# DMA transposes for the q and k of the last four groups, and a different pairing of score blocks from pair 12, in an attention-then-MLP kernel

## The chip, the core and the metric

One core of one Trainium2 chip runs the whole program. The metric is the device time of one execution in microseconds; less is better. TensorE (PE in the profile) does the matrix products, VectorE (DVE), ScalarE (ACT) and GpSimd (POOL) do the elementwise work, and all DMAs are issued by SyncE (SP), whose queue is worked off in order. Each engine runs its own instructions strictly in the order in which they were written; semaphores join the engines.

## What is computed

Attention of two kinds, added, for 8 batches of 8 heads with 576 tokens and head size 64; then an MLP whose activation is h - tanh(h), over 4608 tokens.

```
q_d, k_d, v_d = mean over 4 neighbouring tokens of q, k, v      # 144 coarse tokens
out_d   = softmax(scale * q_d k_d^T) v_d ;  out_up = repeat(out_d, 4)
mask    = |i - j| < 4
out_loc = softmax(where(mask, scale * q k^T, -1e9)) v
x = (out_up + out_loc) as [4608, 512]
h = x @ w_in          # 512 -> 2048
out = (h - tanh(h)) @ w_out    # 2048 -> 512
```

## The kernel before

**Units of work.** Two heads make a pair (p = 0 to 31), two pairs a group (n = 0 to 15), four pairs a batch. The MLP runs over blocks of 512 tokens (kb = 0 to 8) and can begin on a block when the four pairs of its batch or batches have been written into `xT`.

**A group's q and k.** `load_qk` brings them token-major into `qkn` (L345). `reorder` casts them to bf16 into `qr` (L441, q on DVE and k on POOL from group 2 on). `turn(n, i)` (i = 0 for q, 1 for k) then needs the head dimension on the partitions: nine 128x128 transposes on PE (L457) into the PSUM bank pair `ts`, and one ACT copy (L463) from there into `qk`. Two POOL additions (L473, L478) make the coarse version `qkd`. `qr`, `qk` and `qkd` have two buffers each, by n % 2.

**A pair's attention** (`attention(p)`, a generator whose three segments are emitted at different places). `s1` is eight score products of the fine attention in `ts`; `s2` is the two remaining fine ones and four coarse ones. Up to pair 13 they are two PE operations, both in `ts`; from `MERGE` = 14 on one PE operation does `s1` and `s2` of the same pair, `s1` in `ts` and `s2` in the other bank pair `ox`. ACT takes the exponentials (L547 for `s1`, L562 and L565 for `s2`), DVE multiplies by the mask (L551, L569), PE forms the outputs in `ox` (L580, L586), DVE normalises into `ln` (L595, L597). Up to pair 11 PE turns `ln` back (L631 to L635). From `XOUT` = 12 on SP issues a DMA transpose of `ln` into `lnT` (L605; 128 x 896 bf16, seven blocks of 128x128), and DVE adds from there into `xT` (L616).

**The MLP.** `mm1` (L663) and `mm2` (L691) work in four PSUM banks `ps_hy`; ACT's tanh (L672) and DVE's subtraction (L675) lie between them. ACT copies the results (L702) into three buffers `y`, and SP stores them (L705).

**What sets the order.** Nothing is scheduled by hand. `Program` collects the operations with the keys that they read and write, a cost in ns and a priority (lower goes first: attention has 10 or 20 times its number, the MLP's products have 5000). `order()` then plays the program through once with those costs. The latency `LAT` of the producing engine, plus what `spare` adds for late priorities, separates a result from its reader on another engine. The instructions are emitted in the order of these planned starts. So the costs are no work on the chip; they decide the order in which each engine's queue is written, and for a `choice` the engine as well. Where PE is planned to be idle before the first MLP block, a `filler` issues dummy products (L869).

**Loads.** `load_next` runs after each odd pair. A load waits for its buffer and for the key `fl` of pair 2n - `AHEAD`, which the transposes of L605 write, so only loads from about group 9 on wait for it. `vst` has `NVST` = 6 buffers for v, taken by p % 6.

Of the kernel before, what the change touches and what calls it, by code (L numbers as in the profile page):

```python
# [9 lines left out]
BF16 = mybir.dt.bfloat16  # L10
# [5 lines left out]
class Program:  # L16
# [10 lines left out]
    def __init__(self):  # L27
        self.ops = []
        self.alternatives = {}
        self.touch = []  # L30
        self.fresh = set()
        self.spare = (5000, {})
        self.last_write = {}
        self.readers = {}

# [26 lines left out]
    def order(self):  # L62
        n = len(self.ops)
        users = [[] for _ in range(n)]
        left = [0] * n
        for i, (_, _, _, deps, _) in enumerate(self.ops):
            left[i] = len(deps)
            for d in deps:
                users[d].append(i)
        at = [0.0] * n  # L70
        free, ready, start = {}, {}, [None] * n

        def make_ready(i):
            for eng in self.alternatives.get(i, (self.ops[i][0],)):
                ready.setdefault(eng, []).append(i)
        for i in range(n):
            if left[i] == 0:
                make_ready(i)
        for _ in range(n):
            best = None  # L80
            for eng, cand in ready.items():
                if not cand:
                    continue
                now = max(free.get(eng, 0.0), min(at[i] for i in cand))
                if eng == "DMA":
                    pick = min((at[i], i) for i in cand)[1]
                else:
                    pick = min((self.ops[i][4], i) for i in cand if at[i] <= now)[1]
                if best is None or now < best[0]:
                    best = (now, eng, pick)  # L90
            now, eng, i = best
            if i in self.alternatives:
                for other in self.alternatives[i]:
                    ready[other].remove(i)
                self.ops[i] = self.alternatives[i][eng] + self.ops[i][3:]
            else:
                ready[eng].remove(i)
            start[i] = now
            end = now + self.ops[i][1]
            free[eng] = end  # L100
            for u in users[i]:
                same = self.ops[u][0] == eng and eng != "DMA"
                lag = self.LAT[eng]
                if self.spare[0] <= self.ops[u][4] < 5000:
                    lag += self.spare[1].get(eng, 0)
                at[u] = max(at[u], end if same else end + lag)
                left[u] -= 1
                if left[u] == 0:
                    make_ready(u)
        self.start, self.free = start, free  # L110
        return sorted(range(n), key=lambda i: (start[i], i))
# [43 lines left out]
def kernel(  # L155
# [9 lines left out]
    nc = tc.nc  # L165
# [3 lines left out]
    NP = H // 2  # L169
# [4 lines left out]
    A6 = 9  # L174
# [65 lines left out]
        ps_hy.extend(fixed("ps_hy", [128, 512], FP32, 4, pool=pool))  # L240

    P = Program()
    P.spare = (140, {"DMA": 2500, "POOL": 1000})
    op = P.op
    V, A, T, GP = nc.vector, nc.scalar, nc.tensor, nc.gpsimd

# [48 lines left out]
    def load(ns, fn, keys, cost, pri, after=()):  # L295
        op("SP", ns, fn, reads=after, writes=list(keys) + ["queue", ("q", keys[0])],
           pri=pri)
        op("DMA", cost, None, reads=[("q", keys[0])], writes=keys, pri=pri)

    def slot_qk(n):  # L300
        return n % 2 if n >= GV else n % NQKN

    def load_v4(n):

        b, h0 = n // 2, 4 * (n % 2)
        base = v[b, h0]
        for i, (g0, m) in enumerate(((0, 128), (128, 16))):
            rows = bass.AP(tensor=base.tensor, offset=base.offset + 4 * D * g0,
                           ap=[[4 * D, m], [S * D, 4], [1, 4 * D]])
            to = v4[128 - m:128, i]  # L310
            load(650, lambda to=to, rows=rows: nc.sync.dma_start(out=to, in_=rows),
                 [("qkn", 2, i, y) for y in range(2)], (1100, 350)[i], -30,
                 [("fl", 2 * n - AHEAD)])

    def sum_v(n):
# [16 lines left out]
    def load_qk(n):  # L332

        b, h0, s = n // 2, 4 * (n % 2), slot_qk(n)
        for i, src in enumerate((q, k)):
            for y in range(2):
                base = src[b, h0 + 2 * y]
                rows = bass.AP(tensor=base.tensor, offset=base.offset,
                               ap=[[A6 * D, G6], [S * D, 2], [1, A6 * D]])
                t = qkn[s][:, i]  # L340
                to = bass.AP(tensor=t.tensor, offset=t.offset + y * t.ap[0][0],
                             ap=[[2 * t.ap[0][0], G6], t.ap[1], t.ap[2]])

                def issue(to=to, rows=rows):
                    nc.sync.dma_start(out=to, in_=rows)  # L345
                load(650, issue, [("qkn", s, i, y)], T_QK, -30,
                     [("fl", 2 * n - AHEAD)])

    def load_v(p):

        b, j, s = p // NP, p % NP, p % NVST
        t = vst[s]
        for i in range(2):
            h = 2 * j + i
# [22 lines left out]
    def load_w(src, dst, name, f, stage, keys):  # L377

        def issue():
# [4 lines left out]
            else:  # L384
# [4 lines left out]
                else:  # L389
                    nc.sync.dma_start(  # L390
                        out=stage.rearrange("p (c f) -> p c f", c=4),
                        in_=rows[:, 4 * f:4 * f + 4, :])
        load(600, issue, keys, T_W, -30)
        for c in range(4):
            part = stage[c] if isinstance(stage, list) else stage[:, 512 * c:512 * c + 512]
            to = dst[:, c, 512 * f:512 * f + 512] if src is moe_w_in else dst[:, 4 * f + c, :]
# [3 lines left out]


    def prep_v(p):
        s, w, jj = p % NVST, (p // 2) % NVW, p % 2
        P.choice([(eng, ns, lambda fn=fn: fn(  # L404
            out=vw[w][:, 2 * jj:2 * jj + 2, :, 0:64], in_=vst[s]))
                  for eng, ns, fn in CAST_V[p >= NEARLY]],
                 reads=[("vst", s, 0), ("vst", s, 1)],
                 writes=[("vw", w, jj)], pri=10 * p - 12)

    def pool_v(hb):  # L410
# [6 lines left out]
        def mm():  # L417
# [5 lines left out]
        P.fresh.add(len(P.ops))  # L423
        op("PE", 750, mm, reads=[("vw", w, 0), ("vw", w, 1), "pick"],
           writes=[key], pri=pri)
        op("ACT", 300, lambda: A.copy(
            out=vd[w][:, :, :, 0:64],
            in_=pv.rearrange("p w (h d) -> p w h d", d=D)),
           reads=[key], writes=[("vd", w)], pri=pri)
# [16 lines left out]
    def turn(n, i):  # L446
# [4 lines left out]
            ps, ts = po, ox  # L451
        pri, cold = 20 * n, (1.5 if n < 1 else 1.0)
        b16 = ps.rearrange("p n c -> p (n c)").bitcast(BF16)[:, 0:A6 * 128]

        def tr():
            for a in range(A6):
                T.transpose(b16[:, 128 * a:128 * a + 128], qr[s][:, i, a, :], ident)  # L457
        P.fresh.add(len(P.ops))
        op("PE", 480 * cold, tr, reads=[("qr", s, i), "ident"], writes=ts, pri=pri)
        o = qk[s][:, :, KOFF * i:KOFF * i + 576]  # L460

        def copy(fn):
# [13 lines left out]
        def add2(eng):  # L476
            with nc.allow_low_precision("pooled q and k"):
# [3 lines left out]
                 reads=[("qk", s, i)], writes=["half"], pri=pri)  # L481
        P.choice([(name, n2, lambda eng=eng: add2(eng)) for name, _, n2, eng in adders],
                 reads=["half"], writes=[("qkd", s, i)], pri=pri)

    def attention(p):
        b, j, hb, s, jj = p // NP, p % NP, p // 2, p % 2, p % 2
# [41 lines left out]
                             pT[rows, 0, y, :], start=True, stop=True)  # L528
        qks = [("qk", sq, i) for i in range(2)]
        pad = ["bias", "ident"] if first else []  # L530
        yield
        P.fresh.add(len(P.ops))
        if first:
            op("PE", 480, lambda: off(0, 480, 0), reads=pad, writes=ts, pri=pri)
        qkds = [("qkd", sq, i) for i in range(2)]
        if p >= MERGE:
            def both():
                s1()
                s2()
            op("PE", 800, both, reads=qks + qkds, writes=ts + ox, pri=pri)  # L540
        else:
            op("PE", 420 * cold, s1, reads=qks, writes=ts, pri=pri)
        se = p if p < NP else s
        e1 = E[se][:, 0:960].rearrange("p (h c) -> p h c", h=2)
# [3 lines left out]
            out=e1, in_=ps[:, :, 0:480], func=AF.Exp, scale=SCALE),  # L548
           reads=ts, writes=[("E", se, 0)], pri=pri)
        if not first:  # L550
            op("DVE", 700, lambda: V.tensor_tensor(  # L551
                out=e1, in0=e1,
                in1=mask[:, 0:480].unsqueeze(1).to_broadcast([128, 2, 480]),
                op=ALU.mult), reads=["mask"], writes=[("E", se, 0)], pri=pri)
# [1 line left out]
        P.fresh.add(len(P.ops))  # L556
        if first:
            op("PE", 100, lambda: off(480, 96, 0), reads=pad, writes=ts, pri=pri)
        if p < MERGE:
            op("PE", 380 * cold, s2, reads=qks + qkds, writes=ts, pri=pri)  # L560
        sb = ox if p >= MERGE else ts
        op("ACT", 335, lambda: A.activation(  # L562
            out=e2v, in_=pb[:, :, 0:96], func=AF.Exp, scale=SCALE),
# [2 lines left out]
            out=e3, in_=pb[:, :, 96:384], func=AF.Exp, scale=SCALE / 16.0),  # L566
           reads=sb, writes=[("E", se, 2)], pri=pri)
        if not first:
            op("DVE", 220, lambda: V.tensor_tensor(  # L569
                out=e2v, in0=e2v,  # L570
                in1=mask[:, 480:576].unsqueeze(1).to_broadcast([128, 2, 96]),
                op=ALU.mult), reads=["mask"], writes=[("E", se, 1)], pri=pri)
# [109 lines left out]
    def mm2(kb, i):  # L682
# [16 lines left out]
        if part == 3:  # L699
# [5 lines left out]
            op("SP", 600, lambda: nc.sync.dma_start(  # L705
                out=out[r0:r0 + 128, :], in_=y[ys]),
               reads=[("y", ys)], writes=[("yq", ys)], pri=-1)
            op("DMA", 1000, None, reads=[("yq", ys), ("y", ys)], pri=-1)

    def dense(kb):  # L710

# [12 lines left out]
        for i in range(16):  # L724
            if kb < NBLK:
# [2 lines left out]


    M2_FIRST = 16  # L730
    XOUT, T_OUT, AHEAD = 12, 2000, 5
    MERGE, GV = 14, 7
    XADD = [("DVE", (800, 350), V)]
    ORDER, W_FIRST = "g0123", "0123g"
    INNER, OUTER = {4: [0], 5: [1]}, {3: [0, 1], 7: [0, 1]}
    T_QK, T_V, T_W, W_PRI, NEARLY = 760, 800, 2750, 33, NP
    CAST = [("POOL", 700, GP.tensor_copy), ("ACT", 520, A.copy)]
    CAST_V = [[("POOL", 720, GP.tensor_copy), ("ACT", 640, A.copy)],
              [("POOL", 790, GP.tensor_copy)]]
    any3 = [("DVE", 860, V.tensor_copy), ("ACT", 950, A.copy),  # L740
            ("POOL", 1350, GP.tensor_copy)]
    REORDER = [[any3, any3], [any3[0:1], any3[2:3]]]
    TURN = [[("ACT", 1125, A.copy), ("DVE", 1250, V.tensor_copy)],
            [("ACT", 1125, A.copy)]]
    ADDERS = [[("DVE", 750, 440, V), ("POOL", 1190, 750, GP)],
              [("POOL", 1190, 880, GP)]]

    op("DVE", 180, lambda: V.memset(warm, 0.0), writes=["warm"], pri=-999)
# [87 lines left out]
    for p in range(NPAIR):  # L836
# [4 lines left out]
            prep_v(p + 2)  # L841
        if p >= 2:
            next(work[p])
        inner = INNER.get(p, [p % 2] if p >= 2 * NP else [])
        outer = OUTER.get(p, [])
        for i in inner if n + 1 < NGRP else []:
            reorder(n + 1, i)
            turn(n + 1, i)
        next(work[p], None)
        for i in outer:  # L850
            reorder(n + 1, i)
            turn(n + 1, i)
        if p % 2 == 1:
            load_next()
        if p % NP == NP - 1:
# [45 lines left out]
```

## Time and profile before

| what | value |
|---|---|
| median of 6 runs | 345.37 us (344.33 to 346.21) |
| the profiled execution | 344.93 us, span 343.2 us |
| mean granted PE clock in it | 0.984 |
| PE busy | 323.0 us, 94% |
| DVE, ACT, POOL busy | 214.2, 204.6, 152.5 us |
| DMA queue of the loads and stores | 60.1% of the 16 engines' span |
| L663 and L691, both MLP products | 144.2 and 142.0 us busy |
| L457, the transposes of q and k | 252 recorded into `ts`, 19.1 us busy; 36 into `ox`, 3.6 us |

Busy time of a group is the time covered by its instructions from start to end, so groups that overlap are counted in both. PE's instructions are pipelined: the next starts before the one before has ended, and the mean length of an instruction is more than the time it takes from PE. What an instruction takes from PE is read from the distance between starts.

### The profile page before, as it was taken

To read this page: it belongs to the slowest core of one execution; us is meant where nothing else is said; L and a number is where in the kernel's file an instruction comes from. 1 tells how busy PE (TensorE), PEld (TensorE's weight loads), DVE (VectorE), ACT (ScalarE), POOL (GpSimd) and SP (SyncE) were. 2 spreads that over 40 slices of the span, in tenths; PEclk is the share of its full clock that TensorE was granted. 3 is DMA by queue.
4 is the path that set the end of the run, shared out by engine and by line. 5 is a ranking of instruction groups with operands and counts; after the bars stand their busy time and mean duration, and the time that the engine had idled before them with its cause. 6 is when DMAs were issued, how large, how long until landed. Compare 5 with 4: busy or idle time off the path is not lost.

```text
span 343.2 us, 6786 instructions
## 1 busy us (share of the span) xinstructions
PE 323.0 (94%) x2570; PEld 168.6 (49%) x2616; DVE 214.2 (62%) x360; ACT 204.6 (60%) x342; POOL 152.5 (44%) x179
## 2 busy tenths in 40 slices
PE   5977998988999999999999999999999999999995
PEld 1563554554555554555455555454544444444442
DVE  4774765549987678678787568776676453344300
ACT  2685986568868665766666656665765244344411
POOL 8445847595795065839393739493300000000000
PEclk9698999999999999999999999999999999999999
DMA  6999999999902496879878868862222200100021
GB/s 221 269 389 290 273 348 286 270 292 275 265 4 58 127 274 186 215 191 208 226 175 215 185 185 215 227 171 59 59 57 60 57 31 32 61 31 32 31 85 67
DMA packets 84749, 57.51 MB, mean 168 GB/s; under 512 B 62638, under 2 KB 67822, under 8 KB 84718
## 3 DMA queue, kind: packets, MB, share of 16 engines
q1 hardware_dynamic: 84718, 57.09, 60.1%
q8 instruction: 20, 0.33, 0.4%
q14 instruction: 11, 0.09, 0.1%
HBM read 43.05 MB, written 9.44 MB: 153 GB/s over the span
## 4 chain that ended last, share of the span: by engine, by line
PE 80%; DMA 7%; DVE 3%; ACT 3%; SPq 3%; issue 2%; POOL 1%; POOLq 0%; DVEq 0%; ACTq 0%
PE ps_hy L663 34%; PE ps_hy L691 32%; PE ps_ts L457 3%; DMA qkn<-in_q_dram 3%; DMA qkn<-in_k_dram 3%; PE ps_ts L508 3%; PE ps_ox L580 3%; PE ps_ox L586 2%; SPq L345 1%; DMA vst<-in_v_dram 1%; SPq L369 1%; ACT E L547 1%; DVE ln L597 1%; DVE xT L640 1%; PE ps_ox L419 1%
## 5 line engine op out<-in xcount | busy, mean ns | idle before, releaser
L663 PE MATMUL ps_hy<-xT,w_in_sb 128*128 128x512 bf16 x555 | 144.2, 382 | 4.6 <-DVE xT L640 2.7
L691 PE MATMUL ps_hy<-w_out_sb,gT 128*128 128x512 bf16 x552 | 142.0, 379 | 2.4 <-issue 1.1
L675 DVE TENSOR_TENSOR gT<-ps_hy,uy 128x512 bf16<-128x512 f32 x144 | 95.7, 685 | 57.5 <-ACT uy L672 56.7
L672 ACT ACTIVATE uy<-ps_hy 128x512 f32<-128x512 f32 x144 | 83.6, 600 | 78.6 <-PE ps_hy L663 76.6
L663 PEld LDWEIGHTS <-w_in_sb 128*128 128x128 bf16 x576 | 53.7, 98 | 62.7 <-issue 5.9
L691 PEld LDWEIGHTS <-gT 128*128 128x128 bf16 x576 | 53.4, 98 | 60.5 <-issue 1.4
L473 POOL TENSOR_TENSOR half<-qk 128x576 f32<-128x576 bf16 x29 | 34.6, 1195 | 56.8 <-ACT qk L463 55.7
L463 ACT COPY qk<-ps_ts 128x1152 bf16<-128x1152 bf16 x28 | 31.5, 1126 | 14.8 <-PE ps_ts L457 12.6
L702 ACT COPY uy<-ps_hy 128x512 f32<-128x512 f32 x36 | 21.2, 588 | 22.5 <-PE ps_hy L691 20.7
L597 DVE TENSOR_TENSOR ln<-ps_ox,r 128x896 bf16<-128x896 f32 x30 | 32.7, 1089 | 0.9
L547 ACT ACTIVATE E<-ps_ts 128x960 bf16<-128x960 f32 x30 | 29.2, 973 | 6.8 <-PE ps_ts L508 6.7
L404 POOL CAST vw<-vst 128x640 bf16<-128x640 f32 x31 | 24.6, 805 | 10.6 <-DMA vst<-in_v_dram 3.8
L551 DVE TENSOR_TENSOR E<-E,mask 128x960 bf16<-128x960 bf16 x28 | 21.9, 780 | 11.7 <-ACT E L547 11.4
L457 PEld LDWEIGHTS <-qr 128*128 128x128 bf16 x288 | 19.5, 102 | 12.3 <-DVE qr L441 5.5
L322 POOL TENSOR_TENSOR qkn<-qkn 128x512 f32<-128x512 f32 (+1 forms) x18 | 23.9, 1327 | 3.0 <-DMA qkn<-in_v_dram 1.6
L441 DVE CAST qr<-qkn 128x1152 bf16<-128x1152 f32 x18 | 14.2, 790 | 14.7 <-DMA qkn<-in_q_dram 12.2
L478 POOL TENSOR_TENSOR qkd<-half 128x288 bf16<-128x288 f32 x30 | 21.6, 721 | 2.3 <-DVE half L473 1.3
L457 PE MATMUL ps_ts<-ident,qr 128*128 128x128 bf16 x252 | 19.1, 222 | 3.0 <-POOL vd L765 1.5
L441 POOL CAST qr<-qkn 128x1152 bf16<-128x1152 f32 x14 | 17.0, 1218 | 10.3 <-DMA qkn<-in_k_dram 9.8
L616 DVE TENSOR_TENSOR xT<-lnT 128x480 bf16<-128x480 bf16 (+1 forms) x40 | 21.3, 545 | 0.0
L580 PE MATMUL ps_ox<-vw,E 128*128 128x65 bf16 x300 | 18.3, 194 | 1.5 <-DVE E L569 1.5
L595 DVE RECIPROCAL r<-ps_ox 128x14 f32<-128x14 f32 x30 | 7.3, 243 | 19.6 <-PE ps_ox L586 17.7
(86 smaller groups left out, 253.2 us busy)
## 6 DMA issues: line engine op xcount, KB each, us to landing
vst<-in_v_dram SPq DMA_DIRECT2D x62, 160.0 KB, 5.3
qkn<-in_q_dram SPq DMA_DIRECT2D x32, 288.0 KB, 3.4
qkn<-in_k_dram SPq DMA_DIRECT2D x32, 288.0 KB, 5.0
out_dram<-uy SPq DMA_DIRECT2D x36, 256.0 KB, 2.1
qkn<-in_v_dram SPq DMA_DIRECT2D x9, 512.0 KB, 5.0
gT<-in_moe_w_in_dram SPq DMA_DIRECT2D x4, 1024.0 KB, 9.8
xT<-in_moe_w_out_dram SPq DMA_DIRECT2D x8, 256.0 KB, 5.2
gT<-in_moe_w_out_dram SPq DMA_DIRECT2D x2, 1024.0 KB, 10.1
```

The costliest lines, as they stand in the source:

```text
L404: P.choice([(eng, ns, lambda fn=fn: fn(out=vw[w][:, 2 * jj:2 * jj + 2, :, 0:64], in_=vst[s])) for eng, ns, fn in CAST_V[p >= NEARLY]], rea ...
L441: P.choice([(eng, ns, lambda fn=fn: fn(out=dst, in_=srt)) for eng, ns, fn in REORDER[n >= 2][i]], reads=[("qkn", sn, i, x) for x in range(2)],
L457: T.transpose(b16[:, 128 * a:128 * a + 128], qr[s][:, i, a, :], ident)
L463: fn(out=o.rearrange("p y (g a) -> p y g a", a=A6), in_=b16.rearrange("p (a g y) -> p y g a", a=A6, y=2))
L473: eng.tensor_tensor(out=half, in0=four[:, :, :, 0:2], in1=four[:, :, :, 2:4], op=ALU.add)
L547: op("ACT", 980, lambda: A.activation(out=e1, in_=ps[:, :, 0:480], func=AF.Exp, scale=SCALE), reads=ts, writes=[("E", se, 0)], pri=pri)
L580: T.matmul(po[:, hh, 65 * t:65 * t + 65], E[se][:, c:c + 128], vw[w][:, 2 * jj + hh, t, :], start=True, stop=True)
L597: op("DVE", 1090, lambda: V.tensor_tensor(out=ln[sl].rearrange("p n (h d) -> p h n d", d=D), in0=blocks[:, :, :, 0:64], in1=r[s].unsqueeze ...
L663: T.matmul(ps_hy[slot], w_in_sb[:, dc, fc * 128:(fc + 1) * 128], xT[dc][:, kb * 512:kb * 512 + 512], start=(dc == 0), stop=(dc == N_DC - 1))
L672: op("ACT", 490, lambda: A.activation(out=u[us], in_=ps_hy[slot], func=AF.Tanh), reads=[("hy", slot)], writes=[("u", us)], pri=-1)
L675: op("DVE", 620, lambda: V.tensor_tensor(out=gT[g][:, fc, :], in0=ps_hy[slot], in1=u[us], op=ALU.subtract), reads=[("hy", slot), ("u", us) ...
L691: T.matmul(ps_hy[slot], gT[g][:, fc, ts * 128:ts * 128 + 128], w_out_sb[:, fc, :], start=(fc == 0), stop=(fc == N_FF - 1))
```

## The change

It has four parts. Unless said otherwise, the numbers in it are the planner's.

1. For groups n >= `FI` = 12 `turn` has no PE transposes. SP issues a DMA transpose of `qr` (128 x 1152 bf16, nine blocks) into the v buffers `vst[4]` (q) and `vst[5]` (k), read as bf16, and the ACT copy reads from there. For pairs p >= 24 v has only the other four buffers (`slot_v`).
2. `MERGE` = 12, and the PE operation now joins `s1` of pair p+1 with `s2` of pair p. Pair 12's `s1` and pair 31's `s2` stand alone. So the fine scores of a pair are made one pair earlier than before.
3. The turns are placed earlier from pair 12 on (`EARLY`): both of group 7 in pair 12, then q of group (p+3)/2 at the end of each odd pair p and its k in the next even pair. For groups 8 to 11, q's turn then stands, in program order, between the PE operation that has put `s1` of the next pair into `ts` and the exponential that reads `ts`, and it writes `ts`. `AHEAD` is 6.
4. Costs and latencies of the plan are changed: a `spare` by engine, reader and priority; `T_QK` 900, `T_V` 780, `T_OUT` 1600, `W_LATE`, the costs of casts, masks and the copy into `vd`; DVE becomes a third choice for the casts of the weights.

```diff
-    P.spare = (140, {"DMA": 2500, "POOL": 1000})
+    def spare(pri, eng, to):
+        if eng == "DMA":
+            return 2500 if pri >= 140 else 1500 if pri >= 80 else 0
+        level = (pri >= 120) + (pri >= LATER)
+        return SPARE[to == "PE"].get(eng, (0, 0, 0))[level]
+    LATER = 180
+    SPARE = ({"POOL": (0, 500, 1000)},
+             {"POOL": (0, 1000, 1500), "DVE": (0, 300, 800), "ACT": (0, 200, 500)})
...
+    def slot_v(p):
+        return p % 4 if p >= 2 * FI else p % NVST
...
-        op("ACT", 300, lambda: A.copy(
+        op("ACT", 600, lambda: A.copy(
             out=vd[w][:, :, :, 0:64],
...
+        if n >= FI:
+            b16 = vst[4 + i].rearrange("p h t d -> p (h t d)").bitcast(BF16)[:, 0:A6 * 128]
+            ts = [("vst", 4 + i, x) for x in range(2)]
+            op("SP", 900, lambda: nc.sync.dma_start_transpose(
+                out=b16.rearrange("p (a c) -> p a c", a=A6),
+                in_=qr[s][:, i].rearrange("p a c -> p (a c)")),
+               reads=[("qr", s, i)], writes=ts + [("q", ("qT", i))], pri=pri - 60)
+            op("DMA", T_IN, None, reads=[("q", ("qT", i)), ("qr", s, i)], writes=ts,
+               pri=pri)
...
-        P.fresh.add(len(P.ops))
-        op("PE", 480 * cold, tr, reads=[("qr", s, i), "ident"], writes=ts, pri=pri)
+        if n < FI:
+            P.fresh.add(len(P.ops))
+            op("PE", 480 * cold, tr, reads=[("qr", s, i), "ident"], writes=ts, pri=pri)
...
-        if p >= MERGE:
-            def both():
-                s1()
-                s2()
-            op("PE", 800, both, reads=qks + qkds, writes=ts + ox, pri=pri)
-        else:
+        if p <= MERGE:
             op("PE", 420 * cold, s1, reads=qks, writes=ts, pri=pri)
...
-            op("DVE", 700, lambda: V.tensor_tensor(
+            op("DVE", 900, lambda: V.tensor_tensor(
                 out=e1, in0=e1,
...
-        if p < MERGE:
-            op("PE", 380 * cold, s2, reads=qks + qkds, writes=ts, pri=pri)
+        if MERGE <= p < NPAIR - 1:
+            ahead, more = nexts[p + 1]
+
+            def both():
+                ahead()
+                s2()
+            op("PE", 800, both, reads=qks + qkds + more, writes=ts + ox, pri=pri)
+        else:
+            op("PE", 380 * cold, s2, reads=qks + qkds, writes=ox if p >= MERGE else ts,
+               pri=pri)
...
-            op("DVE", 220, lambda: V.tensor_tensor(
+            op("DVE", 450, lambda: V.tensor_tensor(
                 out=e2v, in0=e2v,
...
-    XOUT, T_OUT, AHEAD = 12, 2000, 5
-    MERGE, GV = 14, 7
+    XOUT, T_OUT, AHEAD = 12, 1600, 6
+    MERGE, GV = 12, 7
+    FI, T_IN, EARLY = 12, 2050, 12
...
-    T_QK, T_V, T_W, W_PRI, NEARLY = 760, 800, 2750, 33, NP
-    CAST = [("POOL", 700, GP.tensor_copy), ("ACT", 520, A.copy)]
-    CAST_V = [[("POOL", 720, GP.tensor_copy), ("ACT", 640, A.copy)],
+    W_LATE = [300, 1400, 0, 0]
+    T_QK, T_V, T_W, W_PRI, NEARLY = 900, 780, 2750, 33, NP
+    CAST = [("POOL", 620, GP.tensor_copy), ("ACT", 620, A.copy),
+            ("DVE", 400, V.tensor_copy)]
+    CAST_V = [[("POOL", 790, GP.tensor_copy), ("ACT", 720, A.copy)],
...
-    REORDER = [[any3, any3], [any3[0:1], any3[2:3]]]
+    REORDER = [[any3, any3], [[("DVE", 1150, V.tensor_copy)], any3[2:3]]]
...
-        inner = INNER.get(p, [p % 2] if p >= 2 * NP else [])
-        outer = OUTER.get(p, [])
+        inner = INNER.get(p, [] if p < 2 * NP else [p % 2] if p < EARLY else
+                          [0, 1] if p == EARLY else [1] if p % 2 == 0 else [])
+        m = n + 1 + (p > EARLY)
+        outer = OUTER.get(p, [0] if p > EARLY and p % 2 else [])
...
-        for i in outer:
-            reorder(n + 1, i)
-            turn(n + 1, i)
+        for i in outer if m < NGRP else []:
+            reorder(m, i)
+            turn(m, i)
```

More of the change, by code (lines that the diff above doesn't have):

```diff
@@ L31, in __init__ @@
         self.fresh = set()
-        self.spare = (5000, {})
+        self.spare = lambda pri, eng, to: 0
         self.last_write = {}
@@ L103, in order @@
                 lag = self.LAT[eng]
-                if self.spare[0] <= self.ops[u][4] < 5000:
-                    lag += self.spare[1].get(eng, 0)
+                if self.ops[u][4] < 5000:
+                    lag += self.spare(self.ops[u][4], eng, self.ops[u][0])
                 at[u] = max(at[u], end if same else end + lag)
@@ L242 @@
     P = Program()
-    P.spare = (140, {"DMA": 2500, "POOL": 1000})
+    def spare(pri, eng, to):
[6 more added lines that the diff above has]
+             {"POOL": (0, 1000, 1500), "DVE": (0, 300, 800), "ACT": (0, 200, 500)})
+    P.spare = spare
     op = P.op
@@ L311, in load_v4 @@
             load(650, lambda to=to, rows=rows: nc.sync.dma_start(out=to, in_=rows),
-                 [("qkn", 2, i, y) for y in range(2)], (1100, 350)[i], -30,
+                 [("qkn", 2, i, y) for y in range(2)], (1800, 250)[i], -30,
                  [("fl", 2 * n - AHEAD)])
@@ L345, in issue @@
                     nc.sync.dma_start(out=to, in_=rows)
-                load(650, issue, [("qkn", s, i, y)], T_QK, -30,
+                load(650, issue, [("qkn", s, i, y)],
+                     T_QK + (400 if n == 0 and i == 1 else 0), -30,
                      [("fl", 2 * n - AHEAD)])
     def load_v(p):
-        b, j, s = p // NP, p % NP, p % NVST
+        b, j, s = p // NP, p % NP, slot_v(p)
         t = vst[s]
@@ L392, in issue @@
                         in_=rows[:, 4 * f:4 * f + 4, :])
-        load(600, issue, keys, T_W, -30)
+        load(600, issue, keys, T_W + (W_LATE[f] if src is moe_w_in else 0), -30)
         for c in range(4):
@@ L402, in prep_v @@
     def prep_v(p):
-        s, w, jj = p % NVST, (p // 2) % NVW, p % 2
+        s, w, jj = slot_v(p), (p // 2) % NVW, p % 2
         P.choice([(eng, ns, lambda fn=fn: fn(
@@ L483, in turn @@
                  reads=["half"], writes=[("qkd", s, i)], pri=pri)
+    nexts = {}
     def attention(p):
@@ L530, in attention @@
         pad = ["bias", "ident"] if first else []
+        nexts[p] = s1, qks
         yield
@@ L707, in mm2 @@
                reads=[("y", ys)], writes=[("yq", ys)], pri=-1)
-            op("DMA", 1000, None, reads=[("yq", ys), ("y", ys)], pri=-1)
+            op("DMA", 750, None, reads=[("yq", ys), ("y", ys)], pri=-1)
     def dense(kb):
@@ L741 @@
             ("POOL", 1350, GP.tensor_copy)]
-    REORDER = [[any3, any3], [any3[0:1], any3[2:3]]]
+    REORDER = [[any3, any3], [[("DVE", 1150, V.tensor_copy)], any3[2:3]]]
     TURN = [[("ACT", 1125, A.copy), ("DVE", 1250, V.tensor_copy)],
             [("ACT", 1125, A.copy)]]
-    ADDERS = [[("DVE", 750, 440, V), ("POOL", 1190, 750, GP)],
+    ADDERS = [[("DVE", 760, 440, V), ("POOL", 1190, 850, GP)],
               [("POOL", 1190, 880, GP)]]
```

## The prediction

> **What bounds the kernel.** I read the page's first two parts, then the table of busy time by stretch, PE's waits, and last the timeline around one turn.
>
> ```profile
> span 343.2 us, 6786 instructions
> PE 323.0 (94%) x2570; PEld 168.6 (49%) x2616; DVE 214.2 (62%) x360; ACT 204.6 (60%) x342; POOL 152.5 (44%) x179
> ...
> PE   5977998988999999999999999999999999999995
> ...
> DMA  6999999999902496879878868862222200100021
> ```
>
> The span is PE's: 323.0 us busy and 20.2 us idle. The PE row shows where the idle time lies: in the first ten slices (86 us), while the DMA row stands at 9, and in the last. The table by stretch (PE is the first pair of columns) gives it in us:
>
> ```profile
> 20.00:40.00 20.00, 16.09 (x168) 9.65 (x167) 13.43 (x21) 14.99 (x29) 11.09 (x16) 0.91 1.00 308
> ...
> 60.00:80.00 20.00, 17.13 (x186) 10.23 (x189) 10.74 (x18) 11.61 (x21) 13.12 (x15) 1.00 0.98 274
> ...
> 180.00:200.00 20.00, 19.84 (x158) 10.28 (x160) 14.53 (x25) 12.85 (x21) 12.52 (x14) 1.00 0.76 179
> ```
>
> Over its four stretches of 20 us up to 80 us, PE is busy 15.29 + 16.09 + 18.43 + 17.13 = 66.9, so **13.1 us idle**; from 80 to 320 us **3.3 us**; from 320 to the end 23.2 - 19.4 = 3.8 us, mostly the last copy and store. There are two regimes. Up to 80 us work is missing: it waits for loads and for the first pairs' chains. Afterwards PE has a backlog of MLP products that fills every hole; between 110 and 180 us the view of waits lists 0.2 us for PE. There only one thing counts: **how much time the instructions take from PE**. From 280 us on PE has only MLP products, so later attention costs nothing as long as a backlog is there.
>
> **Part 1, the turns.** Groups 12 to 15 lose 4 x 2 turns of nine transposes. The view of line L457 by stretch has 18 + 18 + 27 + 9 = 72 of them between 180 and 260 us, all in the saturated regime. Their price, from the timeline:
>
> ```profile
> 175.66 0.59 PE L691 MATMUL ps_hy<-w_out_sb,gT 128*128 128x512 bf16 x2
> ...
> 176.09 0.67 PE L457 MATMUL ps_ts<-ident,qr 128*128 128x128 bf16 x9
> ...
> 176.59 1.03 PE L691 MATMUL ps_hy<-w_out_sb,gT 128*128 128x512 bf16 x4
> ```
>
> The row says 0.67 us, but the next product starts 0.50 us after the turn: the rest is pipeline drain under the successor. The turns at 186.02, 204.00 and 209.97 us give 0.50 as well. I take starts: 8 x 0.50 = **4.0 us less on PE**; durations would give 8 x 0.67 = 5.4. [...]
>
> In their place eight DMA transposes go onto SP's queue. The nearest row is that of `lnT`, seven blocks each:
>
> ```profile
> L605 SPq DMA_TRANSPOSE lnT<-ln x20: 1226/1235/1863, 107.8 to 266.5; - x20
> ...
> DMA to landing us min/median/max: 2.9/2.9/5.5
> ```
>
> Nine blocks, in proportion: issue 1.235 x 9/7 = 1.6 us of SP, landing 2.9 x 9/7 = 3.7 us (7.1 at worst). The plan allows 900 ns for the issue, then 2050 + 1800 + 2500 = 6.35 us until ACT's copy, 7.25 in all. So 1.6 + 3.7 = 5.3 us fits even if issue and landing add up, and only the worst landing does not. [...] The row has seven blocks in 2.9 us, 0.41 a block, so I take the row.
>
> The new wait is ACT's copy L463 for a DMA. Behind it in ACT's queue stand tanh L672 and the exponentials. PE goes on until its four MLP banks are full: 4 x 0.86 us (four products of a bank in the chain of waits) = 3.4 us of cover. Behind the transposes on SP stand loads and the stores. A group's issues now take 2 x 1.3 (q, k), 3.9 (v), 1.0 (coarse v), 2 x 1.24 (`lnT`) and some 2 x 0.36 (stores), 10.7 us; with 2 x 1.6 it is 13.9 in about 16.6 us per group (loads at 181.1 and 214.8, two groups). That is tight but fits; after 223 us no loads follow. The ACT copy reads SBUF instead of PSUM; no row has this form. L397 from SBUF takes 616 to 624 ns and L702 from PSUM 588 for the same 128x512, so between -0.04 and +0.04 us a copy, under ACT's 60% load: nothing.
>
> **Parts 2 and 3.** The same score products are done. Blocks of scores on PE go from 22 to 21; one break fewer is between 0 and 0.1 us, which I put at 0. Joining takes the first exponential (L547, 0.97 us) and its mask (0.78) off the chain between block and outputs, so pairs may follow one another faster: no gain while PE is full. The turns of groups 8 to 11 that now write `ts` behind a filled `s1` add a wait of the exponential for 0.50 us of PE; ACT is idle enough to take it. By the code, that exponential then reads what the turn has left in the bank's first 576 columns; this alters numbers, not the count of work. Needing q and k a pair sooner is met by `AHEAD` 6. If pairs slowed down, the backlog would cover it: up to 100 us L691 has loaded 73 weights, 64 for block 0 and 9 for block 1, so 55 x 0.216 = 12 us of block 1 are left, and at 103 us block 2 brings in 128 x 0.216 = 27.6 us.
>
> **Part 4** moves no fixed work, but rewrites the order everywhere, the first 80 us too. Where the plan's costs changed they mostly move to the trace's rows: copy into `vd` 300 to 600 (trace 593), fine mask 220 to 450 (461), ACT cast of weights 520 to 620 (616 to 624), v cast 720 to 790 (805). The stalls that a truer order could shorten are in the view of PE's waits; these four lie before 80 us:
>
> ```profile
> PE ps_hy L663 <- DVE xT L640: 2.7, 2, 1.4
> PE ps_ox L580 <- DVE E L569: 1.5, 1, 1.5
> PE ps_ox L631 <- DVE ln L597: 1.5, 2, 0.9
> ...
> PE ps_ts L508 <- ACT qk L463: 1.1, 1, 1.1
> ```
>
> These sum to 6.8 us. At best about 4 us go; at worst a new order adds 3, the size of two such stalls. The DMA row at 9 says that most cannot go, since what the chains wait for is loads. I take **-1.0 us**, nearer to nothing than to the best.
>
> **Sum.** In the profiled execution 344.93 - 4.0 - 1.0 = 339.9 us; that execution lies 0.44 us under the median, so the median becomes 345.37 - 5.0 = **340.4 us**.
>
> **Rivals.**
> 1. *The turns come off PE, the rest as computed*: 340.4, own range 337.5 to 343.5. For it: 0.2 us of PE waits in 70 us. Chance 0.62.
> 2. *The new order of the front gives the gain back*: +3 there against -4.0 gives 344.4, up to 346 with a further stall in ACT. For it: no stretch up to 80 us is filled, and every queue there is rewritten. Against it: the costs go towards the trace. Chance 0.14.
> 3. *The order gains more than I take*: 6.8 us of stalls mostly gone, 345.37 - 4.0 - 5.0 = 336.4. Against it: DMA at 1.00 from 20 to 60 us. Chance 0.13.
> 4. *Slower: the DMA turns come late on ACT.* An `lnT` transpose or a burst of loads (7.5 us) stands ahead of the turn on SP; ACT stands in its copy, tanh stays behind it, and PE stops when its four banks are full. It decides from an average of 0.50 us of PE stall per turn, that is from 0.50 + 3.4 = 3.9 us of lateness. With 1.3 us of stall per turn: 345.4 - 4.0 - 1.0 + 10.4 = 350.8. For it: SP is filled to 84% of its time, and the plan takes 900 ns for 1.6 us of issue. Against it: the 2.5 us of spare, and two buffers of `qk`, which leave a k turn one and a half pairs between being allowed and being needed, at 8.35 us a pair (L605's 107.8 to 266.5 over 19) 12.5 us. Chance 0.11.
>
> That the transposes do not leave PE is not possible by the code.
>
> **Range and chances.** A difference of 0.3% (1.04 us) is what this kernel's measurement can tell from none: faster is below 344.3, slower above 346.4. Case 1 and case 3 are faster whole (0.75), case 2 a third of the time (0.05): 0.80. The same: 0.07 of case 2, 0.01 of case 4. Slower: 0.02 and 0.10. The range runs from 336.4, the middle of case 3, to 346.0, which takes in all of case 2 but 0.02: some 0.07 is left out below and 0.13 above.
>
> **What would show it.** L457 has 216 transposes instead of 288 and none after about 185 us; DMA_TRANSPOSE has 28 issues. Right: PE's busy time falls by about 4 us, its idle time from 80 to 320 us stays under 4 us, and the idle time up to 80 us is between 9 and 16 us. ACT's waits for the transposes should come to little, their landing to 3 to 5 us. Wrong: `ps_hy` L663 or L691 waiting for ACT or DVE between 180 and 270 us while ACT waits for `vst` (rival 4), or a front that is longer by 3 us (rival 2). [...]

## The result, and the profile after

The changed kernel takes 341.51 us (median of 17 runs) beside 345.27 us (median of 38) for the kernel before; the forecast was 340.4 us. The medians are of all runs, while the ratio, 0.9875 with a 95% interval of 0.985 to 0.990, compares fast runs alone (six of the 17 took over 1.5% longer than the fastest). It means 1.25% or 4.3 us less, inside the range and 0.7 us short of the forecast of 5.0. The size was right; its make-up was not.

The page of the changed kernel, its first lines and the PE and DMA rows:

```profile
span 340.3 us, 6679 instructions
...
PE 321.1 (94%) x2509; PEld 165.0 (48%) x2552; DVE 233.4 (69%) x369; ACT 206.2 (61%) x334; POOL 157.1 (46%) x178
...
PE   7777999999999999999998999999999999999995
...
DMA  6999999989921989996999999942232000100021
```

Two things stand out against the rows of before. PE is full from the fifth slice on, where it was at 8 to 9 up to the tenth. And there is a new dent near the middle, at an 8. The table by stretch (the first pair is PE) shows both in us:

```profile
60.00:80.00 20.00, 19.68 (x206) 11.97 (x207) 13.28 (x21) 14.40 (x23) 13.18 (x15) 1.00 0.94 260
...
180.00:200.00 20.00, 17.71 (x148) 8.94 (x150) 17.69 (x25) 15.93 (x25) 13.58 (x14) 1.00 1.20 242
200.00:220.00 20.00, 19.04 (x138) 9.21 (x140) 18.89 (x28) 11.73 (x19) 10.91 (x11) 1.00 0.96 243
```

The kernel before has for the last of these stretches:

```profile
200.00:220.00 20.00, 19.74 (x169) 10.26 (x171) 14.89 (x25) 12.67 (x21) 11.89 (x12) 1.00 0.87 228
```

From 60 to 80 us PE's idle time went from 2.9 to 0.3 us. From 180 to 220 us it is 2.29 + 0.96 = 3.25 us, where it was 0.16 + 0.26 = 0.42. That is where the DMA turns are. The views of their two lines say what is in them:

```profile
L470 SPq DMA_TRANSPOSE vst<-qr x8: 1291/2048/2556, 166.2 to 222.8; - x8
...
DMA to landing us min/median/max: 4.0/4.6/6.6
```

```profile
L486 ACT COPY qk<-ps_ts x18: 1113/1123/1167, 43.3 to 160.7; 128x1152 bf16<-128x1152 bf16 x18
...
L486 ACT COPY qk<-vst x8: 2184/2198/2275, 174.5 to 233.7; 128x1152 bf16<-128x1152 bf16 x8
```

The transposes land after 4.6 us at the median, inside the 3 to 5 us foretold. But the same ACT copy (minimum, median, maximum in ns) takes 2198 from SBUF where it takes 1123 from PSUM. What that does is seen in the timeline of one stall. ACT, DVE and PE, each in order of start, with length, line and operation:

```profile
178.05 2.20 ACT L486 COPY qk<-vst 128x1152 bf16<-128x1152 bf16 x1 [0.84 <-POOL half L496]
180.14 1.08 ACT L701 ACTIVATE uy<-ps_hy 128x512 f32<-128x512 f32 x2
181.11 0.34 ACT L591 ACTIVATE E<-ps_ox 128x192 bf16<-128x192 f32 x1
```

```profile
180.77 1.29 DVE L704 TENSOR_TENSOR gT<-ps_hy,uy 128x512 bf16<-128x512 f32 x2 [2.24 <-ACT uy L701]
181.97 0.76 DVE L645 TENSOR_TENSOR xT<-lnT 128x96 bf16<-128x96 bf16 x1
182.66 1.22 DVE L454 CAST qr<-qkn 128x1152 bf16<-128x1152 f32 x1
183.79 0.77 DVE L598 TENSOR_TENSOR E<-E,mask 128x192 bf16<-128x192 bf16 x1
```

```profile
179.09 0.38 PE L533 MATMUL ps_ts<-qk 64*128 64x120 bf16 x8
...
182.11 1.02 PE L692 MATMUL ps_hy<-xT,w_in_sb 128*128 128x512 bf16 x4 [0.64 <-DVE gT L704]
...
184.62 0.20 PE L609 MATMUL ps_ox<-vw,E 128*128 128x65 bf16 x1 [0.92 <-DVE E L598]
```

The scores were on PE from 179.09 us, in groups of 0.2 to 0.4 us. ACT stood in its copy until 178.05 + 2.20 = 180.25, and two tanh came before the exponential. DVE idled 2.24 us and then had its whole queue to do before the mask. PE waited 0.64 us for a bank and 0.92 us for the mask. In this one stall the length of the copy is not all: ACT first idled 0.84 us until POOL's addition L496, which reads q's half of the same buffer `qk`, was done. That is the only time ACT idled before any of the eight copies, so none of them waited for its DMA.

**Counting PE's work.** To see where time comes from, I count the weight loads that PE has issued up to a moment and give each the PE time read between starts: 0.2155 us for an MLP product (0.86 for four), 0.0555 for a transpose (0.50 for nine, while one of L457 lasts 222 ns in the mean), 0.48 for a block of 14 score products, 0.53 for 18 output products (most blocks of the kernel before show 0.56, 0.03 a pair, which hardly enters the gains), 0.11, 0.05 and 0.15 for the few others of the first 100 us, nothing for dummies. "Gain" below is against the kernel before, in us of work; kernels with DMA turns have 4.0 us less to do in all.

| kernel | work by 100 us (gain) | work 100 to 260 us (gain) | 4.0 for the turns | sum | span (gain) |
|---|---|---|---|---|---|
| before | 73.6 | 156.2 | | | 343.2 |
| changed | 76.3 (+2.7) | 152.1 (-4.1) | +4.0 | +2.6 | 340.3 (+2.9) |
| a1, PE turns | 74.9 (+1.3) | 155.7 (-0.5) | | +0.8 | 341.4 (+1.8) |
| a2, DMA turns only | 73.0 (-0.6) | 152.3 (-3.9) | +4.0 | -0.5 | 343.3 (-0.1) |
| a4, copy planned at 2200 | 75.8 (+2.2) | 154.7 (-1.5) | +4.0 | +4.7 | 338.2 (+5.0) |
| b1, costs only | 76.6 (+3.0) | 149.9 (-6.3) | | -3.3 | 346.8 (-3.6) |
| b2, old costs | 72.4 (-1.2) | 146.9 (-9.3) | +4.0 | -6.5 | 349.4 (-6.2) |
| b3, copy on POOL | 76.2 (+2.6) | 151.7 (-4.5) | +4.0 | +2.1 | 340.3 (+2.9) |
| b4, blocks 288 bytes apart | 77.6 (+4.0) | 152.5 (-3.7) | +4.0 | +4.3 | 338.5 (+4.7) |
| c1, turns in ox | 76.0 (+2.4) | 154.9 (-1.3) | +4.0 | +5.1 | 337.6 (+5.6) |
| c2, costs, old spare | 76.8 (+3.2) | 155.2 (-1.0) | | +2.2 | 341.4 (+1.8) |
| c3, POOL planned at 2400 | 77.7 (+4.1) | 150.9 (-5.3) | +4.0 | +2.8 | 340.0 (+3.2) |
| d1, c1 with PE turns | 78.0 (+4.4) | 155.5 (-0.7) | | +3.7 | 339.7 (+3.5) |

Each row is one profiled execution. The sums agree with the spans to within 1 us (a3, below, is the exception: -22.0 against -25.6), so the split is good to about that.

The first column must be read with its spread. In the traces of a1, a3, a4, b1, b3, b4, c1, c3 and d1 all five engines have their instructions in the changed kernel's order up to 100 us, and yet their gains by then run from 1.3 to 4.4 us. They go with the clock that PE was granted from 20 to 40 us: 1.3 to 2.7 at 0.83, 2.6 and 3.0 at 0.91, 4.0 to 4.4 at 1.00 (a3: 1.5 at 0.74). In the same way the kernel before, a2 and b2 have one order up to there and stand at 73.6, 73.0 and 72.4. The two orders do not overlap, and their means, 76.4 and 73.0, are some 3 us apart: that is what the new order gains in front, and differences within one order say nothing of a change. The second column is steadier: b4, whose order is the changed kernel's to the end, has -3.7 beside -4.1.

So in the changed kernel **the DMA turns' 4.0 us are lost again between 100 and 260 us (-4.1), and the gain is that of the first 100 us (+2.7)**. The experiments test that.

### The profile page after: what moved, and what is told of

It reads as the page before. It is cut to its first block, busy times and chain, and to the rows that moved or that the text cites. A ratio compares the mean times of both kernels' runs of the same rounds, so it can differ in the third digit from the quotient of the medians.

```text
span 340.3 us, 6679 instructions
## 1 busy us (share of the span) xinstructions
PE 321.1 (94%) x2509; PEld 165.0 (48%) x2552; DVE 233.4 (69%) x369; ACT 206.2 (61%) x334; POOL 157.1 (46%) x178
## 4 chain that ended last, share of the span: by engine, by line
PE 73%; DVE 10%; issue 4%; SPq 4%; ACT 3%; POOL 2%; DMA 2%; POOLq 0%; ACTq 0%; DVEq 0%
PE ps_hy L720 32%; PE ps_hy L692 30%; PE ps_ts L479 3%; DVE gT L704 3%; PE ps_ts L533 2%; PE ps_ox L609 2%; DMA gT<-in_moe_w_in_dram 2%; SPq L382 2%; ACT qk L486 2%; PE ps_ox L615 2%; DVE ln L626 2%; DVE xT L645 2%; SPq L357 1%; DVE E L572 1%; DVE xT L669 1%
## 5 line engine op out<-in xcount | busy, mean ns | idle before, releaser
L720 PE MATMUL ps_hy<-w_out_sb,gT 128*128 128x512 bf16 x557 | 139.4, 379 | 1.1 <-issue 0.2
L496 POOL TENSOR_TENSOR half<-qk 128x576 f32<-128x576 bf16 x28 | 33.1, 1184 | 45.4 <-ACT qk L486 34.3
L572 DVE TENSOR_TENSOR E<-E,mask 128x960 bf16<-128x960 bf16 x28 | 25.3, 905 | 4.1 <-ACT E L568 3.9
L454 POOL CAST qr<-qkn 128x1152 bf16<-128x1152 f32 x17 | 22.6, 1330 | 9.9 <-DMA qkn<-in_k_dram 6.1
L645 DVE TENSOR_TENSOR xT<-lnT 128x480 bf16<-128x480 bf16 (+1 forms) x40 | 26.0, 671 | 0.0
L486 ACT COPY qk<-ps_ts 128x1152 bf16<-128x1152 bf16 x18 | 20.3, 1126 | 8.8 <-PE ps_ts L479 7.3
L598 DVE TENSOR_TENSOR E<-E,mask 128x192 bf16<-128x192 bf16 x28 | 15.9, 568 | 7.3 <-ACT E L591 7.3
L609 PEld LDWEIGHTS <-E 128*128 128x128 bf16 x300 | 15.6, 98 | 8.7 <-DVE E L598 1.9
L486 ACT COPY qk<-vst 128x1152 bf16<-128x1152 bf16 x8 | 17.7, 2209 | 0.8 <-POOL half L496 0.8
L479 PEld LDWEIGHTS <-qr 128*128 128x128 bf16 x216 | 13.7, 100 | 7.8 <-DVE qr L454 2.2
```

The costliest lines, as they stand in the source:

```text
L486: fn(out=o.rearrange("p y (g a) -> p y g a", a=A6), in_=b16.rearrange("p (a g y) -> p y g a", a=A6, y=2))
L496: eng.tensor_tensor(out=half, in0=four[:, :, :, 0:2], in1=four[:, :, :, 2:4], op=ALU.add)
L572: op("DVE", 900, lambda: V.tensor_tensor(out=e1, in0=e1, in1=mask[:, 0:480].unsqueeze(1).to_broadcast([128, 2, 480]), op=ALU.mult), reads= ...
L609: T.matmul(po[:, hh, 65 * t:65 * t + 65], E[se][:, c:c + 128], vw[w][:, 2 * jj + hh, t, :], start=True, stop=True)
L645: up=up: eng.tensor_tensor(out=xo[:, QW * t0:QW * t0 + nt * n].rearrange("p (t g a) -> p t g a", t=nt, a=4), in0=lnT[sl][:, t0:t0 + nt, 0: ...
L720: T.matmul(ps_hy[slot], gT[g][:, fc, ts * 128:ts * 128 + 128], w_out_sb[:, fc, :], start=(fc == 0), stop=(fc == N_FF - 1))
```

## The experiments

**a1 and a2: the DMA turns taken out of the changed kernel, and put alone into the kernel before.**

```diff
-    FI, T_IN, EARLY = 12, 2050, 12
+    FI, T_IN, EARLY = 16, 2050, 12
```

> The changed kernel with PE's turns kept for all groups (FI = 16), all else as changed. My theory (the DMA turns are worth 4.0 us of PE, and their ACT copies, 2.2 us each instead of 1.1, give back some 2.8 us in stalls between 180 and 220 us): 341.5 + 4.0 - 2.8 = 342.7 us, and PE's idle time from 180 to 220 us falls from 3.3 us to under 1. Rival A (these stalls come from the new order, not from the DMA turns): they stay, 345.5 us. Rival B (the DMA turns bring nothing, the whole gain is the new order): 341.5 us.

Measured: 341.68 us, ratio 0.9878 (0.983 to 0.9925). Idle time from 180 to 220 us is 0.3 us, so the stalls do belong to the DMA turns. But the time is that of the changed kernel: rival B (my theory's 342.7 us stands at the edge of the interval).

a2 is the kernel before with `slot_v` and the branch `n >= FI` of `turn`.

> The kernel before with only the DMA turns of groups 12 to 15 (and the four v buffers from pair 24). My theory: 345.3 - 4.0 = 341.3 us without stalls, up to 344.1 with the whole 2.8 us of them, and ACT's copy from SBUF again near 2.2 us. Rival A (stalls belong to the new order): 341.3 us, PE idle under 1 us from 180 to 220 us. Rival B: 345.3 us.

Measured: 345.4 us, ratio 0.9992 (0.996 to 1.002), against 346.0 us on the same chip. Rival B again. Its table by stretch:

```profile
180.00:200.00 20.00, 18.34 (x136) 8.97 (x138) 13.51 (x23) 15.58 (x21) 13.50 (x14) 1.00 0.84 212
...
240.00:260.00 20.00, 18.07 (x139) 8.90 (x139) 13.87 (x26) 13.89 (x23) 2.95 (x4) 1.00 0.30 61
```

From 180 to 260 us PE idles 4.9 us, where it was 0.9 before: 4.0 us of turns saved, 4.0 us of stalls. As it was made, the DMA part is worth nothing that can be told from 0 in either surrounding (a2's interval is some 1.1 us to each side).

**a4: the plan is told how long the copy is.** Groups from 12 get their own entry in `TURN`.

```diff
-            [("ACT", 1125, A.copy)]]
+            [("ACT", 1125, A.copy)], [("ACT", 2200, A.copy)]]
...
-for eng, ns, fn in TURN[n >= 2]]
+for eng, ns, fn in TURN[(n >= 2) + (n >= FI)]]
```

> The changed kernel, with the plan told that the ACT copy of a DMA turn takes 2200 ns instead of 1125; the instructions are the same, their order may differ. If the stalls come from the plan not knowing the copy's length: PE's idle time from 180 to 220 us falls from 3.3 to 1 us or less, 339 us. If they come from the length itself, or from something else (rival A): 341 to 342 us.

Measured: 339.52 us, ratio 0.9797 (0.976 to 0.984), with copies still at 2206 ns. PE's waits from 160 to 240 us, first of the changed kernel, then of a4 (us in total, times, longest):

```profile
PE ps_ox L609 <- DVE E L598: 1.5, 2, 0.9
PE ps_hy L692 <- DVE gT L704: 0.9, 2, 0.6
PE ps_hy L692 <- DVE xT L645: 0.4, 1, 0.4
PE ps_hy L692 <- ACT uy L731: 0.2, 1, 0.2
```

```profile
PE ps_hy L692 <- issue: 0.5, 3, 0.2
PE ps_hy L720 <- issue: 0.3, 2, 0.2
```

So it is not the length of the copy as such, which ACT can bear, but that the plan did not know it: the exponentials and tanh behind the copy were placed as if it took half as long. With the right number the order is another and the DMA turns pay. One better order could be chance; c1 and c3 below speak to that.

**a3 and b4: why the copy is slow.**

```diff
# a3, q: 
+                fn(out=o.rearrange("p y (g a) -> p y a g", a=A6),
+                   in_=b16.rearrange("p (a g y) -> p y a g", a=A6, y=2))
# a3, k:
+                fn(out=o.rearrange("p y (g a) -> p a g y", a=A6),
+                   in_=b16.rearrange("p (a g y) -> p a g y", a=A6, y=2))
```

> The changed kernel, the ACT copy of the DMA turns walked in another order: q in rows of g (it reads every second element and writes every ninth), k as the source lies in SBUF (it reads in sequence, and writes the two heads in turn). If the 256-byte stride of the reads makes the copy slow, one or both fall from 2.2 to about 1.1 us; if it is SBUF as the source, both stay at 2.2. My theory then gives 338.7 to 340.1 us for fast copies, since the stalls at 180 to 220 us go. Rival A (the copies' length does not matter): 341.5 us either way.

Measured: 370.75 us, ratio 1.072 (1.067 to 1.077). The view of `qk` in a3:

```profile
L490 ACT COPY qk<-vst x4: 5267/5282/5316, 175.6 to 251.1; 128x1152 bf16<-128x1152 bf16 x4
L493 ACT COPY qk<-vst x4: 5513/5518/5561, 182.2 to 259.3; 128x1152 bf16<-128x1152 bf16 x4
```

Both theories missed. k now reads SBUF in sequence and takes 5.5 us, and q reads in steps of 4 bytes and takes 5.3. Both now write in steps, so two-byte writes in steps of 18 bytes, or in turn to two rows, cost more than reads in steps of 256 bytes (2.2 us). The eight copies are 8 x 5.40 - 8 x 2.21 = 25.5 us longer on ACT, and the time rises by 29.2: here ACT's length does reach PE.

> The changed kernel with the nine blocks of a DMA turn 144 elements apart in SBUF instead of 128, so that the copy reads with a stride of 288 bytes instead of 256. If the stride of 256 bytes is what makes the copy take 2.2 us: about 1.1 us and 339 us in all. If any strided read of two-byte elements from SBUF is that slow: 2.2 us and 341.5 us.

(b4 builds the blocks' access pattern with a step of 144 elements for both the transpose and the copy.) Measured: copy 2298 ns, 340.9 us, ratio 0.9884 (0.985 to 0.992). The stride of 256 bytes in itself is not it. What is shown is that this two-byte copy in steps takes 2.20 us from SBUF with steps of 256 bytes and 2.30 with 288, and 1.12 from PSUM with 256. Why SBUF is the slower source for the same steps, no run shows. Nor is it shown whether short steps would help: a3's reads in sequence and in steps of 4 bytes came with writes in steps, and the copy from SBUF with such reads and with writes in sequence was not run.

**b3 and c3: the copy on POOL.**

```diff
-            [("ACT", 1125, A.copy)]]
+            [("ACT", 1125, A.copy)], [("POOL", 1350, GP.tensor_copy)]]   # 2400 in c3
```

> The changed kernel with the copies of the eight DMA turns on POOL instead of ACT (planned at 1350 ns). If ACT's 17.7 us of copies are what stalls PE from 180 to 220 us: the stalls go, 338.5 us. If POOL is as slow on these reads or too full (62% in that stretch): the additions behind the copy come later, the stalls stay or grow, 341 to 344 us.

> The changed kernel with the copies of the DMA turns on POOL, planned at 2400 ns (they took 2.36 us there). If the plan's knowledge of the length is what matters: 338 to 339.5 us, as with ACT planned at 2200 (339.5). If POOL is too full for them: 340 to 342 us.

Measured: b3 339.92 us, ratio 0.9841 (0.980 to 0.988); c3 341.02 us, ratio 0.9874 (0.983 to 0.992). POOL needs 2360 and 2196 ns (medians) for it. In b3 the stalls stay, so freeing ACT alone does not remove them. PE idles 1.25 + 1.69 us from 180 to 220 us:

```profile
180.00:200.00 20.00, 18.75 (x154) 9.26 (x153) 18.59 (x26) 11.11 (x20) 18.45 (x15) 1.00 1.20 224
200.00:220.00 20.00, 18.31 (x137) 8.80 (x137) 19.93 (x24) 9.56 (x17) 19.54 (x17) 1.00 0.96 226
```

c3, with the truer plan, is no faster and fell into the range given for a full POOL, but its trace shows another reason. From 180 to 220 us PE idles 0.16 + 0.80 = 1.0 us, so most of the stalls did go:

```profile
180.00:200.00 20.00, 19.84 (x171) 10.05 (x173) 18.75 (x27) 12.19 (x22) 19.04 (x16) 1.00 1.08 213
200.00:220.00 20.00, 19.20 (x141) 9.28 (x142) 19.32 (x26) 10.14 (x18) 17.20 (x15) 1.00 1.05 237
```

The execution loses 3.0 us from 140 to 160 us, where its order is still the changed kernel's. PE waits there for ACT, and ACT for POOL:

```profile
PE ps_ts L533 <- ACT qk L486: 2.7, 1, 2.7
```

```profile
ACT qk L486 <- POOL half L496: 3.6, 1, 3.6
```

ACT's copy of k waited for POOL's addition of q, as in the stall shown above. The plan does not count this wait, since it has separate keys for q's and k's halves of `qk`. The addition itself stood behind work on coarse v that had waited 3.56 us for its load. After the stall PE's granted clock was 0.50 from 148 to 150 us (0.96 in the mean from 140 to 180 us). Whether all six runs of c3 lose time there is not known.

What the plan's number does can now be read over five orders. With the true length PE idles 0.6 us (a4), 0.7 (c1) and 1.0 (c3) from 180 to 220 us; with a length that is too short it idles 3.25 (changed; 2.7 in b4, the same order) and 2.9 (b3).

**b1, b2 and c2: the plan's costs and the pairing, each alone.**

> The kernel before with part 4 alone: the changed costs and latencies of the plan, nothing else. My theory now (the gain is the plan's truer costs, the DMA turns give back on ACT what they take from PE): about 341.7 us, as with PE's turns in the changed kernel, and more of PE's work done by 100 us. Rival (the gain is the new pairing of score blocks and the earlier turns): 345.3 us.

> The changed kernel with the old costs and latencies of the plan: parts 1 to 3 alone. My theory: nothing left of the gain, 345 to 346 us. Rival (pairing and earlier turns): 341.5 us.

Measured: b1 348.88 us, ratio 1.011 (1.0085 to 1.014); b2 351.08 us, ratio 1.015 (1.012 to 1.018). Both theories missed: **each half is slower alone, and only together do they gain**. b1 has the whole gain of the first 100 us (+3.0) and loses 6.3 after it. b2 has none in front, where its order is that of the kernel before, and loses 9.3 after it. Its longest PE wait is for a copy that the plan thought done:

```profile
PE ps_ts L523 <- ACT qk L476: 7.2, 5, 2.3
```

A score block that now wants the next group's q and k a pair earlier stands on PE for 7.2 us when the order was made with the old costs and latencies.

c2 is b1 with the old `spare`:

> The kernel before with part 4 except the latencies: only the costs of the operations are the new ones, spare is the old one. The costs alone with the new latencies were at 348.9 us; they had 3.0 us more of PE's work done by 100 us and lost 6.3 us of it between 100 and 260 us. If the longer latencies, with the old pairing of the score blocks, make that loss: it goes, and the front's gain stays, 342.5 us. If the costs make it: 348 to 349 us. If the front's gain comes from the latencies: 345.5 us.

Measured: 343.69 us against 344.77, ratio 0.998 (0.995 to 1.001). The loss after 100 us falls from 6.3 to 1.0, the front's +3.2 stays. So the longer latencies, together with the old pairing, made b1's loss, and the front's gain comes from the costs. The median moves by 1.1 us only, less than the 1.8 of the profiled execution and the 2.3 that I expected, so how much the front's gain is worth alone is not settled beyond "1 to 3 us" (the ratio's interval even takes in 0).

**c1 and d1: the bank of the early q turns.** In the changed kernel the exponential of pairs 14, 16, 18 and 20 reads, by the code, what the turn left in `ts`, and the trace shows it for the first: it has `s1` of pair 14 at 125.28 us, the turn into the same bank at 125.77, the exponential at 126.66. So the fine scores of one head and part of the other are not used in these four pairs. The order of work is unaffected, but a repair must be priced. c1 is a4 with those turns in `ox`, free after the pair before has been normalised:

```diff
-        if n in (1, 2):
+        if n in (1, 2) or (8 <= n < FI and i == 0):
             ps, ts = po, ox
```

> The changed kernel with the copy planned at 2200 ns, and the q turns of groups 8 to 11 in ox instead of ts, so that the exponentials of pairs 14, 16, 18 and 20 read their own scores. If the sharing of ts costs or gains nothing: 339.5 us (ratio 0.980), as with ts. If the turn in ox holds up the next block, which needs ox too: up to 4 x 1 us more, 343.5 us.

Measured: 338.35 us, ratio 0.9814 (0.978 to 0.985). Repairing costs nothing measurable, and c1 is the fastest of all: 6.4 us less than before.

d1 is c1 with `FI` = 16, so PE turns all groups and eight q turns go into `ox`.

> The best version so far (copy planned at 2200 ns, q turns of groups 8 and later in ox) with PE's turns kept for all groups (FI = 16). If the DMA turns are worth their 4.0 us once the plan knows the copy's length: ratio to the kernel before 0.990 to 0.993, 341.5 to 342.5 us, against 0.981. If the better plan alone made the difference: 0.981, 338.4 us.

Measured: 343.92 us, ratio 0.9991 (0.996 to 1.002). This is slower than either theory. The DMA turns are worth 0.9991 - 0.9814 = 1.8% or 6 us between d1 and c1, and 0.9878 - 0.9797 = 0.8% or 2.8 us between a1 and a4 (about 0.6 to 5 with both intervals); the 4.0 computed lies between. Part of d1's loss must be of another kind, since d1 is slower than a1, which differs only in the bank. The profiled execution of d1, its fastest at 341.41 us, does not show it; this stays open.

## Why the prediction was right, point by point

**What bounds it** held: in all rows of the table, PE's work done by 260 us gives the span to within 1 us.

**Part 1.** The price of a turn on PE, 0.50 us between starts, held: 72 transposes fewer (216 on PE, none after 185 us, as foretold), and a2 saves about what its stalls then cost. PE's busy time fell by 1.9 us (323.0 to 321.1) where the sum had about 4. The landing was 4.6 us at the median where the sum had 3.7; issue 2.05 where it had 1.6. Together, 6.65 us, they were inside the plan's allowance of 7.25; a block took 0.51 us to land where the row of L605 had 0.41. What failed is the sentence "between -0.04 and +0.04 us a copy [...]: nothing". It took a float32 cast read in sequence as the nearest row for a bf16 copy read in steps, whose length from SBUF no row of before shows. The copy went up by 1.08 us, eight times, and the net of part 1 was nothing instead of 4.0. Rival 4 had the right engine and the right path (ACT in its copy, tanh and exponentials behind it, PE at full banks) with the wrong cause: nothing landed late. (A slip that changes nothing: the loads at 181.1 and 214.8 make 16.9 us a group, not 16.6, and SP 82% full.)

**Part 4** was under-sized: +2.7 us by 100 us in the changed kernel, and about 3 as the mean of the kernels with this order, where I had taken 1.0. The spread from +1.3 to +4.4 goes with PE's granted clock.

**Parts 2 and 3** were put at 0 because they move no work. That is true of work and false of order: adding them to the new costs takes 348.88 to 341.68 us (b1 to a1; ratios 1.011 and 0.988), 7 to 8 us. Pricing a plan's costs and its structure one by one was the wrong form of sum, since each is slower without the other.

So the forecast's 5.0 us stood on 4.0 that were given back and 1.0 that was in fact larger: two errors in opposite directions, and the total came out right by luck. The named idle times show it: from 80 to 320 us I had allowed up to 4 us, and it was 5.3; up to 80 us it was 9.6, in the range given.

## What to carry to other kernels

Work that is taken off the bounding engine is worth its time only if the replacement has the length that the order was made for; read the new instruction's length in the first trace and put it back into the plan before judging the idea (here about 0 became 3 to 6 us). The copy's price here went with where and in what steps it reads and writes (1.12 us from PSUM, 2.20 from SBUF with the same steps, 5.28 and 5.52 with writes in steps), so a row with another memory or another step is not a near row. And when order comes from a planner, costs and structure have to be tested together: either alone can be slower.

## What the runs showed of the hardware that was not expected

- An ACT copy of 128 x 1152 bf16 in steps of 256 bytes: 1.12 us from PSUM, 2.20 from SBUF, 2.30 with steps of 288 bytes. Writing SBUF in steps of 18 bytes took 5.28 us, and with the innermost write alternating between two rows of a partition 5.52, though the read was in sequence. GpSimd took 2.36 (b3) and 2.20 us (c3) at the median for the same copy.
- Nine 128x128 blocks by DMA transpose land 4.6 us after issue, beside loads (4.0 to 6.6). The transposes of seven blocks went from 2.9 to 3.5 us at the median in the changed kernel.
